# Loads, square roots and transposes of the first chunk rearranged in a fused layer-norm, S5 and SwiGLU kernel

## The chip, the cores and the metric

The kernel runs on one core of one Trainium2 chip. The metric is the device time of one execution in microseconds (us), and lower is better. Before the change it takes 180.79 us (median of 3 runs, 180.5 to 180.87).

Engine names follow the profile. PE is TensorE (the matmuls), PEld is its weight load, DVE is VectorE, ACT is ScalarE, POOL is GpSimd and SP is SyncE, which here only issues DMAs.

## The reference, cut to what matters

```python
x  = A_x                      # 1 x 2048 x 512, bf16
xn = (x - mean) / sqrt(var + 1e-5)            # layer norm over the 512 columns
# S5: a diagonal complex state-space model with 512 states
Bu = xn @ B_bar.T                             # complex
h[t] = Lam_bar * h[t-1] + Bu[t]               # scan over the 2048 rows
a  = 2 * real(h @ C.T) + xn * Dskip
# SwiGLU with 1376 hidden columns
b  = (silu(xn @ w_gate) * (xn @ w_up)) @ w_down
return x + a + b
```

All arrays are bf16. Nothing can start before some rows of x are normalised and transposed, and the first matmuls also need `w_gate`. The subject here is how this start is arranged, and what a start that comes half a microsecond sooner is worth 170 us later.

## The kernel before

The rows are cut into 4 chunks of 512, and each chunk into 4 tiles of 128 rows. Chunk 0 is special. Its tiles are normalised in halves of 256 columns, each half is transposed on PE, ACT copies it out of PSUM, and the gate matmuls of six column tiles follow tile by tile ("quarters"). Every later chunk is normalised as a whole and transposed by DMA. The weights have 512 rows, which the matmuls sum over; a K slice is 128 of these rows.

A list scheduler in the program fixes the order of ACT, DVE and POOL ahead of time. An `order=` argument forces one task behind another. PE and SP keep the order of the program. The traces show DVE and ACT keeping to their lists: in the kernel before ACT's square root of tile 1, whose data were ready at 6.09, came at 6.52, behind two evacuations.

The loads, the layer norm of chunk 0, its transposes and its gate matmuls:

```python
x_load(0)                                          # 128 KB, SP
act_q = [x_load(1, eng="act")]                     # ACT's first DMA issue
act_q.append(wg_load(0, eng="act", order=(act_q[-1],)))   # gate weights, K slices 0 and 1, 384 KB
x_load(2)
wg_load(1)                                         # K slices 2 and 3
x_load(3)
...  # [cut] parameters, w_up, the rest of w_gate, x tiles 4-7

def ln_chunk0():
    last = bn_half(0, 0)                           # statistics of 256 columns
    for a in range(4):
        last = bn_half(a, 1, order=(last,))
        last = g.add("dve", ... bn_aggr ..., order=(last,))
        hold["sd"] = g.add("act", ... Sqrt(var + eps) ...)
        if a < 3:
            last = bn_half(a + 1, 0, order=(last,))
        last = g.add("dve", ... reciprocal(sd0) -> rstd ..., order=(last,))
        for h in range(2):
            last = ln_half(a, h, order=(last,))    # xn = (x - mean) * rstd, 256 columns
    ...  # [cut]

def xt_tile_fine(a, hs=(0, 1)):
    for h in hs:
        ...  # [cut] PE: two 128 x 128 transposes of xn
        ...  # [cut] ACT: copy of 128 x 256 from PSUM to xnT ("evacuation")

def ffn_gate_quarters(pairs):
    ...  # [cut]
    pe_warm(10, 512, wbank)                        # matmuls on constants ("warm-up")
    ln_chunk0()
    xt_tile_fine(0, (0,)); pe_warm(1, 256, wbank)
    xt_tile_fine(0, (1,)); pe_warm(3, 128, wbank)
    for q in range(4):                             # tile q of the chunk
        if q < 3:
            steps = [(i, bk, 2 * kh, 2 * kh + 2) for kh in range(2) for i, bk in tiles]
        ...  # [cut]
        for n, (i, bk, k0, k1) in enumerate(steps):
            if q < 3 and n in (8, 10):             # transposes of the next tile
                xt_tile_fine(q + 1, ((n - 8) // 2,))
            ...  # [cut] params_t at q == 3, n == 4; then the matmuls of this step
```

Part of the later chunks:

```python
def loads_stage_b2():
    dma("ld_cre", CT[:, 0], A_C_re, ..., xpose=True)      # the program lets a transposing load wait for all DMAs before it,
    dma("ld_cim", CT[:, 1], A_C_im, ..., xpose=True)      # and every later load wait for it
    dma("ld_x8", x_sb[:, 8:12, :], ...)                   # x tiles 8-11, that is chunk 2
    ...  # [cut] w_down, x tiles 12-15, Dskip

def ln_apply_act(a0):                                     # chunks 2 and 3
    g.add("dve", ... nmr = -mean * rstd ...)              # rstd comes from POOL
    for a in range(a0, a0 + 4):
        g.add("act", ... xn = rstd * x + nmr ...)         # four ACT instructions of 0.7 us
```

## Time and profile before

| reading (profiled run, 180.54 us) | before |
|---|---|
| span, PE busy | 178.8 us, 174.8 us (98%) |
| x0 and x1 land | 3.34, 3.53 us |
| first gate weight piece lands (its last landing record) | 6.61 us |
| first gate matmul starts | 6.75 us |
| normalisation of tiles 0, 1, 2, 3 starts on DVE | 4.92, 7.04, 8.78, 10.52 us |
| first 512-wide matmul starts (called F below) | 13.37 us |
| last matmul of the kernel starts | 176.25 us |

Part 1 and part 4 of the page (busy time of each engine with its share of the span and its instructions; then the chain that ended last, by engine):

```profile
span 178.8 us, 2391 instructions
PE 174.8 (98%) x917; PEld 83.6 (47%) x925; DVE 161.9 (91%) x280; ACT 89.5 (50%) x116; POOL 9.9 (6%) x21
...
PE 95%; DMA 1%; DVE 1%; issue 1%; ACT 0%
```

PE is the bound, and it is nearly full. The only time to be had lies where PE is not yet at its work, in the first 13 us. The chain of waits, cut to that stretch, has the start, the duration and what was done; its last line continues to 20 us:

```profile
0.79 2.54 DMA x_sb<-in_A_x_dram
...
6.24 0.39 ACT xnT L552
6.64 0.11 issue
6.75 1.05 PE pb L760 x16
...
13.54 6.47 PE pb L715 x30
```

Read naively, it says that the first gate matmul at 6.75 waited for ACT's evacuation. The timeline of the same stretch (start, duration, engine, line, operation, output from input, and in brackets the idle time before and what ended it) is more exact:

```profile
4.72 0.16 DVE L519 RECIPROCAL rstd<-sd 128x1 f32<-128x1 f32 x1
...
5.82 0.81 ACT L552 ACTIVATE xnT<-pb 128x256 bf16<-128x256 bf16 x2 [1.13 <-PE pb L546]
...
6.52 0.29 ACT L515 ACTIVATE sd<-mv,epst 128x1 f32<-128x1 f32 x1
...
6.75 0.55 PE L760 MATMUL pb<-xnT,wg 128*128 128x128 bf16 x7 [0.22 <-ACT xnT L552]
...
7.04 0.34 DVE L505 TENSOR_SCALAR xn_sb<-x_sb,mv,rstd 128x256 bf16<-128x256 bf16 x1
```

The gate matmuls of chunk 0 end where the first 512-wide matmul starts:

```profile
13.37 5.34 PE L715 MATMUL pb<-xnT,wu 128*128 128x512 bf16 x24
```

Two things are to be seen. The two evacuations began at 5.82, and the first of them is all that the first matmuls need. It ended at 6.20, and they started at 6.75. And ACT did the square root of tile 1 (6.52) only behind both evacuations, so the normalisation of tile 1 began at 7.04, 2.12 us behind that of tile 0.

What else arrived late was the weights. The trace has 16 landing records for the first weight piece, read here as one for each of the 16 DMA engines, in us:

```
4.68 4.70 4.71 4.73 4.74 4.75 4.77 4.78 4.79 4.81 4.82 4.83 4.85 4.92   6.13   6.61
```

Fourteen of them lie at 4.92 or before, and the last two came 1.2 and 1.7 us later. PE's first gate matmul started at 6.75, behind the last of the 16 records (6.61) and not behind the fourteenth (4.92), although the evacuation that it needs had ended at 6.20.

### The profile page before, as it was taken

How to read it: one execution, taken by the hardware profiler on the slowest of the kernel's cores; microseconds unless marked ns; L12 is line 12 of the kernel's file. 1: busy time of each engine (PE TensorE's matmuls, PEld its weight loads, DVE VectorE, ACT ScalarE, POOL GpSimd, SP SyncE). 2: the span in 40 equal slices, each digit the busy share in tenths (PEclk: the TensorE clock that was granted, in tenths of full speed). 3: DMA queues.
4: the chain of work that ended last, by engine and by line, in shares of the span. 5: the costliest groups of instructions: out<-in, count | busy, mean ns of one | idle time of the engine just before them, and what ended most of it. 6: DMA issues, size and time to landing. Idle time of an engine off the chain costs nothing.

```text
span 178.8 us, 2391 instructions
## 1 busy us (share of the span) xinstructions
PE 174.8 (98%) x917; PEld 83.6 (47%) x925; DVE 161.9 (91%) x280; ACT 89.5 (50%) x116; POOL 9.9 (6%) x21
## 2 busy tenths in 40 slices
PE   8999999999999999999999999999999999999994
PEld 2694444443444444444444444444444444444743
DVE  2859884798799999999999999999999999999983
ACT  3469898989899947006655651000965620000000
POOL 3013400001300000040000000000000000000000
PEclk9999999999999999999999999999999999999999
DMA  5994669469460000002330000001100000000122
GB/s 177 350 340 110 87 134 107 90 172 354 123 117 4 0 0 0 0 4 87 78 71 0 0 0 4 0 0 59 59 0 4 0 0 0 0 0 4 59 86 90
DMA packets 22882, 12.37 MB, mean 69 GB/s; under 512 B 15096, under 2 KB 22872, under 8 KB 22872
## 3 DMA queue, kind: packets, MB, share of 16 engines
q1 hardware_dynamic: 22456, 11.70, 25.4%
q10 hardware_dynamic: 416, 0.52, 0.9%
q8 instruction: 7, 0.11, 0.3%
q14 instruction: 3, 0.02, 0.0%
HBM read 6.46 MB, written 2.10 MB: 48 GB/s over the span
## 4 chain that ended last, share of the span: by engine, by line
PE 95%; DMA 1%; DVE 1%; issue 1%; ACT 0%
PE pb L715 36%; PE pb L915 21%; PE pb L832 15%; PE pb L928 15%; PE pb L760 3%; PE pb L795 2%; DMA x_sb<-in_A_x_dram 1%; PE pb L805 1%; PE pb L546 1%; DVE st L500 0%; ACT xnT L552 0%; DVE xn_sb L505 0%; ACT sd L515 0%; DVE x_sb L933 0%; DVE mv L513 0%
## 5 line engine op out<-in xcount | busy, mean ns | idle before, releaser
L872 DVE TENSOR_TENSOR_SCAN rot<-sm,car,rot 128x512 bf16<-128x512 f32 x32 | 39.0, 1266 | 0.1
L915 PE MATMUL pb<-wd,hT 128*128 128x512 bf16 (+3 forms) x194 | 38.1, 355 | 0.2
L715 PE MATMUL pb<-xnT,wu 128*128 128x512 bf16 x160 | 37.3, 379 | 0.0
L715 PE MATMUL pb<-xnT,wg 128*128 128x512 bf16 x136 | 32.0, 379 | 0.0
L928 PE MATMUL pb<-W,hss 128*128 128x512 bf16 (+2 forms) x140 | 28.1, 355 | 0.2
L832 PE MATMUL pb<-xnT,BT 128*128 128x512 bf16 x128 | 28.1, 379 | 0.0
L915 PEld LDWEIGHTS pb<-wd,hT 128*128 128x128 bf16 (+1 forms) x198 | 18.5, 98 | 19.9
L715 PEld LDWEIGHTS pb<-xnT,wu 128*128 128x128 bf16 x160 | 15.6, 98 | 18.7 <-ACT uf L785 0.3
L727 ACT ACTIVATE sg<-pb 128x1024 bf16<-128x1024 f32 x20 | 20.2, 1023 | 7.7 <-PE pb L715 7.6
L785 ACT ACTIVATE uf<-pb 128x1024 bf16<-128x1024 f32 x20 | 20.4, 1026 | 7.0 <-PE pb L715 5.3
L715 PEld LDWEIGHTS pb<-xnT,wg 128*128 128x128 bf16 x136 | 13.2, 98 | 16.4 <-issue 0.8
L928 PEld LDWEIGHTS pb<-W,hss 128*128 128x128 bf16 x144 | 13.4, 98 | 14.3
L832 PEld LDWEIGHTS pb<-xnT,BT 128*128 128x128 bf16 x128 | 12.5, 98 | 15.1
L839 ACT ACTIVATE u_sb<-pb 128x1024 bf16<-128x1024 f32 x16 | 16.4, 1025 | 4.9 <-PE pb L832 4.5
L787 DVE TENSOR_TENSOR hT<-sg,uf 128x1024 bf16<-128x1024 bf16 x20 | 13.3, 677 | 0.4 <-ACT uf L785 0.3
L863 DVE TENSOR_TENSOR rot<-u_sb,cosT 128x2048 bf16<-128x2048 bf16 x8 | 9.7, 1216 | 2.9 <-ACT cosT L676 2.9
L933 DVE TENSOR_TENSOR x_sb<-pb,x_sb 128x512 bf16<-128x512 f32 (+2 forms) x18 | 10.8, 623 | 1.4 <-PE pb L928 1.4
L814 ACT ACTIVATE sg<-pb 96x1024 bf16<-96x1024 f32 x2 | 2.0, 1020 | 17.3 <-PE pb L795 17.3
L494 ACT ACTIVATE xn_sb<-x_sb,nmr,rstd 128x512 bf16<-128x512 bf16 x8 | 5.9, 803 | 8.9 <-DVE nmr L491 8.9
L863 DVE TENSOR_TENSOR rot<-rot,cosT 128x2048 bf16<-128x2048 bf16 x8 | 9.7, 1215 | 0.1
L863 DVE TENSOR_TENSOR rot<-rot,sin 128x2048 bf16<-128x2048 bf16 x8 | 9.7, 1216 | 0.0
L863 DVE TENSOR_TENSOR rot<-u_sb,sin 128x2048 bf16<-128x2048 bf16 x8 | 9.7, 1214 | 0.0
(76 smaller groups left out, 143.0 us busy)
## 6 DMA issues: line engine op xcount, KB each, us to landing
out_dram<-x_sb SPq DMA_DIRECT2D x15, 128.0 KB, 1.7
x_sb<-in_A_x_dram SPq DMA_DIRECT2D x3, 512.0 KB, 7.5
wd<-in_B_w_down_dram SPq DMA_DIRECT2D x1, 1280.0 KB, 7.0
wu<-in_B_w_up_dram SPq DMA_DIRECT2D x1, 768.0 KB, 5.6
wg<-in_B_w_gate_dram SPq DMA_DIRECT2D x1, 608.0 KB, 6.9
wu<-in_B_w_up_dram SPq DMA_DIRECT2D x1, 608.0 KB, 8.0
x_sb<-in_A_x_dram SPq DMA_DIRECT2D x3, 128.0 KB, 2.7
wg<-in_B_w_gate_dram ACTq DMA_DIRECT2D x1, 384.0 KB, 5.4
```

The lines of the kernel that those rows point to most:

```text
L494: g.add("act", lambda e, a=a: e.activation(out=xn_sb[:, a % NXN, :], in_=x_sb[:, a, :], func=AF.Identity, scale=rstd[:, a:a + 1], bias=nmr ...
L715: inst = e.matmul(pbank[0:fs, bk, :].rearrange("p (j t) -> p j t", j=4), lhsT=w[:, kt, i * 128:i * 128 + fs], rhs=xnT[:, c % 2, :, kt, :], ...
L727: g.add("act", lambda e: e.activation(out=sg[rows, sl, 0:n, :].rearrange("p a t -> p (a t)"), in_=pair_f32(rows, bk, 512 * n), func=AF.Sil ...
L785: g.add("act", lambda e: e.activation(out=uf[rows, ul, 0:n, :].rearrange("p a t -> p (a t)"), in_=pair_f32(rows, bk, 512 * n), func=AF.Ide ...
L787: g.add("dve", lambda e: e.tensor_tensor(out=hT[rows, hb, i0:i0 + n, :], in0=sg[rows, sl, 0:n, :], in1=uf[rows, ul, 0:n, :], op=ALU.mult), ...
L832: inst = e.matmul(pbank[:, bk, :].rearrange("p (j t) -> p j t", j=4), lhsT=BT[:, ri, kt, pt * 128:(pt + 1) * 128], rhs=xnT[:, c % 2, :, kt ...
L839: g.add("act", lambda e: e.activation(out=u_sb[:, us].rearrange("p r t -> p (r t)"), in_=pair_f32(slice(0, 128), b0), func=AF.Identity), r ...
L863: tt = lambda out, a, b, op, r, w, nm: g.add("dve", lambda e: e.tensor_tensor(out=out, in0=a, in1=b, op=op), reads=r, writes=w, name="%s_% ...
L872: g.add("dve", lambda e, A0=A0, A1=A1, k=k, ri=ri, pt=pt: e.tensor_tensor_scan(out=A1[:, k, ri, :], data0=rr[:, pt:pt + 1].to_broadcast([1 ...
L915: inst = e.matmul(pbank[:, bk, 0:nc_], lhsT=hT[0:fs, hb, i, lt * 128:(lt + 1) * 128], rhs=wd[0:fs, i, c0:c0 + nc_], start=(i == 0), stop=F ...
L928: inst = e.matmul(pbank[:, bk, 0:nc_], lhsT=hss[:, hb, pt, ri, lt * 128:(lt + 1) * 128], rhs=W12[:, ri, pt, c0:c0 + nc_], start=False, sto ...
L933: g.add("dve", lambda e, bk=bk, a=a, c0=c0, nc_=nc_: e.tensor_tensor(out=x_sb[:, a, c0:c0 + nc_], in0=pbank[:, bk, 0:nc_], in1=x_sb[:, a, ...
```

## The change

The change is meant to start the gate matmuls sooner and to keep DVE, ACT and PE from waiting for each other in chunk 0. Its parts are these.

- Loads: SP issues x0, x1 and x2, one after the other. The weights come in three K pieces of 384, 192 and 192 KB. ACT first issues a tiny load (the "touch", a few values from 16 partitions of the weights) and then the first two pieces; SP issues the third, behind x2.
- Tile 0 gets its statistics in one pass of 512 columns, not two of 256. The loop around it is only written differently.
- The square root of the next tile stands ahead of the evacuation of the second half.
- The transposes of tiles 2 and 3 come two steps earlier among the gate matmuls, and those of tile 1 are placed for the three K pieces.
- The transpose of the parameters moves into tile 3's transposes, and its copy from DVE to ACT.

```diff
-        x_load(0)
-        act_q = [x_load(1, eng="act")]
-        act_q.append(wg_load(0, eng="act", order=(act_q[-1],)))
-        x_load(2)
-        wg_load(1)
+        x_load(0)
+        x_load(1)
+        act_q = [dma("ld_touch", tch[0:16], wg_v[0:128:8, :, 0:2], [("tch",)], 16 * 16, eng="act")]
+        act_q.append(wg_load("a0", 0, 2, eng="act", order=(act_q[-1],)))
+        x_load(2)
+        act_q.append(wg_load("a1", 2, 3, eng="act", order=(act_q[-1],)))
+        wg_load("a2", 3, 4)
         x_load(3)
 ...
         def ln_chunk0():
-            last = bn_half(0, 0)
+            last = ln_stat0(0, (bn_full(0),))           # 512-wide pass, aggregate, square root
+            last = bn_half(1, 0, order=(last,))
             for a in range(4):
-                last = bn_half(a, 1, order=(last,))
-                ... bn_aggr, Sqrt, bn_half(a + 1, 0) ...
                 last = ... reciprocal ...
                 for h in range(2):
                     last = ln_half(a, h, order=(last,))
+                if a < 3:
+                    last = bn_half(a + 1, 1, order=(last,))
+                    last = ln_stat0(a + 1, (last,))     # aggregate, square root
+                if a < 2:
+                    last = bn_half(a + 2, 0, order=(last,))
 ...
                 hold["evac"] = g.add("act", evac, ...,
+                                     order=(hold["sd%d" % (a + 1)],) if h and a < 3 else ())
 ...
-            pe_warm(10, 512, wbank)
+            pe_warm(9, 512, wbank)
+            pe_warm(2, 128, wbank)
 ...
-                    if q < 3 and n in (8, 10):
-                        xt_tile_fine(q + 1, ((n - 8) // 2,))
+                    if q < 3 and n in ((12, 15) if q == 0 else (6, 8)):
+                        xt_tile_fine(q + 1, (0 if n in (6, 12) else 1,))
 ...  # [cut] the parameter transposes, and a repair of the scheduler's priorities
```

More of the change, by code (lines that the diff above doesn't have):

```diff
@@ L90, in _schedule @@
         t.lat = (_DMA_LAT + t.nbytes / _DMA_BW) if t.dma else 0.0
-    for t in reversed(tasks):
+    nin = defaultdict(int)
+    for t in tasks:
+        for d in succ[t]:
+            nin[d] += 1
+    for d in chain_next.values():
+        nin[d] += 1
+    topo = [t for t in tasks if nin[t] == 0]
+    for t in topo:
+        for d in succ[t] + ([chain_next[t]] if t in chain_next else []):
+            nin[d] -= 1
+            if nin[d] == 0:
+                topo.append(d)
+    for t in reversed(topo):
         b = 0.0
@@ L319, in bass_parallel_sum__ssm_conv_s5__swiglu_ffn__prompt_kernel @@
         epst = sb("epst", [128, 1], F32)
+        tch = sb("tch", [16, KT, 2], B16)
         praw = sb("praw", [128, 3, PT], B16)
@@ L396, in bass_parallel_sum__ssm_conv_s5__swiglu_ffn__prompt_kernel, with pload, wg_load @@
         FH0 = 6 * 128
-        def pload(name, slot, src):
-            return dma(name, prow[4 * slot:4 * slot + 4, :], src.rearrange("(a p) -> a p", p=128), [("prow", slot)], 1024)
+        def pload(name, slot, src, **kw):
+            return dma(name, prow[4 * slot:4 * slot + 4, :], src.rearrange("(a p) -> a p", p=128), [("prow", slot)], 1024, **kw)
         def x_load(a, **kw):
             return dma("ld_x%d" % a, x_sb[:, a:a + 1, :], x_v[:, a:a + 1, :], [("x", a)], TILEB, **kw)
-        def wg_load(h, **kw):
-            return dma("ld_wgA%d" % h, wg[:, 2 * h:2 * h + 2, 0:FH0], wg_v[:, 2 * h:2 * h + 2, 0:FH0], [("wg", "a%d" % h)], 256 * FH0 * 2, **kw)
+        def wg_load(nm, k0, k1, **kw):
+            return dma("ld_wg" + nm, wg[:, k0:k1, 0:FH0], wg_v[:, k0:k1, 0:FH0], [("wg", nm)], (k1 - k0) * 128 * FH0 * 2, **kw)
         x_load(0)
-        act_q = [x_load(1, eng="act")]
-        act_q.append(wg_load(0, eng="act", order=(act_q[-1],)))
+        x_load(1)
+        act_q = [dma("ld_touch", tch[0:16], wg_v[0:128:8, :, 0:2], [("tch",)], 16 * 16, eng="act")]
+        act_q.append(wg_load("a0", 0, 2, eng="act", order=(act_q[-1],)))
         x_load(2)
-        wg_load(1)
+        act_q.append(wg_load("a1", 2, 3, eng="act", order=(act_q[-1],)))
+        wg_load("a2", 3, 4)
         x_load(3)
@@ L459, in pe_warm @@
             g.add("pe", mm, writes=BK(bk), name="pe_warm", est=n * w * 0.84, ninst=n)
-        def params_t(slot):
-            g.add("pe", lambda e: e.transpose(out=ptr[:, slot, 0:12], in_=prow[:], identity=ident[0:12, 0:12]),
-                  reads=[("prow", k) for k in range(3)] + [("ident",)], writes=BK(slot), name="parT", est=60)
-        def params_ev(slot, order):
-            return g.add("dve", lambda e: e.tensor_copy(out=praw[:].rearrange("p k a -> p (k a)"), in_=ptr[:, slot, 0:12]),
-                         reads=BK(slot), writes=[("praw", k) for k in range(3)], name="parTev", est=80, order=order)
         def bn_st(a, order=()):
@@ L500, in bn_half @@
             return g.add("dve", lambda e: e.bn_stats(out=st0[:, a, h, :], in_=x_sb[:, a, h * 256:(h + 1) * 256]),
-                         reads=[("x", a)], writes=[("st0", a, h)], name="bnst%d_%d" % (a, h), est=330, order=order)
+                         reads=[("x", a)], writes=[("st0", a, h)], name="bnst%d_%d" % (a, h), est=350, order=order)
         def ln_half(a, h, order=()):
@@ L505, in ln_half @@
             return g.add("dve", lambda e: e.tensor_scalar(out=xn_sb[:, a % NXN, cs], in0=x_sb[:, a, cs], scalar1=mv[:, a, 0:1], scalar2=rstd[:, a:a + 1],
-                                                          op0=ALU.subtract, op1=ALU.mult),
-                         reads=[("x", a), ("mv", a), ("rstd", a)], writes=[("xh", a, h)] + ([("xn", a % NXN)] if h else []), name="xn%d_%d" % (a, h), est=220, order=order)
+                                                        op0=ALU.subtract, op1=ALU.mult),
@@ new lines, in ln_half, with ln_stat0 @@
+                         reads=[("x", a), ("mv", a), ("rstd", a)], writes=[("xh", a, h)], name="xn%d_%d" % (a, h), est=300, order=order)
+        def ln_stat0(a, order):
+            t = g.add("dve", lambda e: e.bn_aggr(out=mv[:, a, :], in_=st0[:, a].rearrange("p h s -> p (h s)")[:, 0:6 if a == 0 else 12]),
+                      reads=[("st0", a, 0), ("st0", a, 1)], writes=[("mv", a)], name="bnag%d" % a, est=160, order=order)
+            hold["sd%d" % a] = g.add("act", lambda e: e.activation(out=sd0[:, a:a + 1], in_=mv[:, a, 1:2], func=AF.Sqrt, bias=epst[:, 0:1]),
+                                     reads=[("mv", a), ("epst",)], writes=[("sd0", a)], name="sd%d" % a, est=280)
+            return t
@@ L509, in ln_chunk0, with bn_full @@
         def ln_chunk0():
-            last = bn_half(0, 0)
+            def bn_full(a, order=()):
+                return g.add("dve", lambda e: e.bn_stats(out=st0[:, a, 0, :], in_=x_sb[:, a, :]), reads=[("x", a)], writes=[("st0", a, 0)], name="bnst%d" % a, est=640, order=order)
+            last = ln_stat0(0, (bn_full(0),))
+            last = bn_half(1, 0, order=(last,))
             for a in range(4):
-                last = bn_half(a, 1, order=(last,))
-                last = g.add("dve", lambda e, a=a: e.bn_aggr(out=mv[:, a, :], in_=st0[:, a].rearrange("p h s -> p (h s)")),
-                             reads=[("st0", a, 0), ("st0", a, 1)], writes=[("mv", a)], name="bnag%d" % a, est=130, order=(last,))
-                hold["sd"] = g.add("act", lambda e, a=a: e.activation(out=sd0[:, a:a + 1], in_=mv[:, a, 1:2], func=AF.Sqrt, bias=epst[:, 0:1]),
-                                   reads=[("mv", a), ("epst",)], writes=[("sd0", a)], name="sd%d" % a, est=280)
-                if a < 3:
-                    last = bn_half(a + 1, 0, order=(last,))
@@ L519, in ln_chunk0 @@
                 last = g.add("dve", lambda e, a=a: e.reciprocal(out=rstd[:, a:a + 1], in_=sd0[:, a:a + 1]), reads=[("sd0", a)], writes=[("rstd", a)],
-                             name="rstd%d" % a, est=100, order=(last,))
+                             name="rstd%d" % a, est=140, order=(last,))
                 for h in range(2):
                     last = ln_half(a, h, order=(last,))
+                if a < 3:
+                    last = bn_half(a + 1, 1, order=(last,))
+                    last = ln_stat0(a + 1, (last,))
@@ L541, in xt_tile_fine, with tr2 @@
                 slot = xt_pair[0] + h
-                def tr2(e, h=h, slot=slot):
+                par = a == 3 and h == 1
+                def tr2(e, h=h, slot=slot, par=par):
+                    if par:
+                        e.transpose(out=ptr[:, slot, 512:524], in_=prow[:], identity=ident[0:12, 0:12])
                     for j in range(2):
@@ L548, in tr2 @@
                     return inst
-                g.add("pe", tr2, reads=[("xh", a, h), ("ident",)], writes=BK(slot), name="xT%d_%d" % (a, h), est=2 * 64, ninst=2)
+                g.add("pe", tr2, reads=[("xh", a, h), ("ident",)] + [("prow", k) for k in range(3) if par], writes=BK(slot), name="xT%d_%d" % (a, h), est=2 * 64 + 100 * par, ninst=2 + par)
                 def evac(e, h=h, slot=slot):
@@ L553, in evac @@
                                         in_=ptr[:, slot, 0:256].rearrange("p (k t) -> p k t", k=2), func=AF.Identity)
-                hold["evac"] = g.add("act", evac, reads=BK(slot), writes=[("xnTh", a, h)] + ([("xnT", 0, a % 4)] if h else []), name="xTev%d_%d" % (a, h), est=340)
+                if par:
+                    g.add("act", lambda e, slot=slot: e.activation(out=praw[:].rearrange("p k a -> p (k a)"), in_=ptr[:, slot, 512:524], func=AF.Identity),
+                          reads=BK(slot), writes=[("praw", k) for k in range(3)], name="parTev", est=200, order=(hold["evac"],))
+                hold["evac"] = g.add("act", evac, reads=BK(slot), writes=[("xnTh", a, h)] + ([("xnT", 0, a % 4)] if h else []), name="xTev%d_%d" % (a, h), est=340,
+                                     order=(hold["sd%d" % (a + 1)],) if h and a < 3 else ())
         def xt_chunk_dma(c):
@@ L562, in resid_chunk @@
             s0 = (4 * c) % NXN
-            xr = [("xn", s0 + j) for j in range(4)]
+            xr = [("xn", s0 + j) for j in range(4)] + ([("xh", j, h) for j in range(4) for h in range(2)] if c == 0 else [])
             xx = [("x", 4 * c + j) for j in range(4)]
@@ L700, in wres @@
             if nm == "wg" and i < 6:
-                return [("wg", "a0"), ("wg", "a1")]
+                return [("wg", "a0"), ("wg", "a1"), ("wg", "a2")]
             return [(nm, 0 if i < 6 else 1)]
@@ L749, in ffn_gate_quarters @@
             for q in range(4):
-                if q < 3:
+                if q == 0:
+                    steps = [(i, bk, 0, 2) for i, bk in tiles] + [(i, bk, k, k + 1) for k in (2, 3) for i, bk in tiles]
+                elif q < 3:
                     steps = [(i, bk, 2 * kh, 2 * kh + 2) for kh in range(2) for i, bk in tiles]
@@ L762, in mm @@
                         return inst
-                    hs = range(k0 // 2, k1 // 2)
-                    if q == 3 and n == 4:
-                        params_t(xt_pair[0])
-                        params_ev(xt_pair[0], (hold["xn3"],))
-                    g.add("pe", mm, reads=[("wg", "a%d" % h) for h in hs] + [("xnTh", q, h) for h in hs], writes=BK(bk), name="mm_gq%d_%d_%d" % (i, q, k0),
+                    hs = range(k0 // 2, (k1 + 1) // 2)
+                    g.add("pe", mm, reads=[("wg", "a%d" % max(k - 1, 0)) for k in range(k0, k1)] + [("xnTh", q, h) for h in hs], writes=BK(bk), name="mm_gq%d_%d_%d" % (i, q, k0),
                           est=(k1 - k0) * 56, ninst=k1 - k0)
```

## The prediction

> **What bounds the kernel now.** Page, part 1: PE is busy 174.8 of 178.8 us (98%). The chain of waits is 95% PE; the list of PE's waits shows none after 20 us. So only the start can be shortened. The timeline: first gate matmul at 6.75, first up matmul at 13.54 by the chain, and from there PE runs back to back to the end.
>
> **What gates the first matmul.** The chain names ACT's evacuation of xnT (6.24 + 0.39). I doubt this: the first gate matmuls need only the first half, and that evacuation began at 5.82 and took 0.384. The landing records of the first weight load (384 KB, issued on ACT at 1.22) say something else: 14 of its 16 DMA engines finish by 4.92, one at 6.13 and one at 6.61; PE's semaphore event follows at 6.64. At the end its packets trickle beside the other queue's. [...] So the gate is the weight's last two engines, at 6.6.
>
> **What the change does.**
> 1. Loads. x1 moves to SyncE, a tiny touch takes ACT's first issue (0.4 us), so weights still start near 1.2; K slices 2 and 3 are split (192 KB each), slice 2 behind slices 0 and 1 in the same queue. Fewer bytes on SyncE compete with the first piece: I expect it at 4.9 to 5.9.
> 2. Tile 0 statistics in one 512-wide pass: 0.615 (later chunks: 2.46 for four) for 0.76, and a shorter aggregate: 0.2 us sooner. From the trace's steps: normalised half 4.71, transpose 5.2, evacuation 5.61 to 5.99, first matmul about 6.1, 0.65 sooner, if the weights are there.
> 3. Square root of tile 1 ahead of the second evacuation: before it waited from 6.09 to 6.52 for ACT. Tile 1's xn starts at about 6.44, was 7.04. The second half of xnT is ready at 6.5, needed at 6.8.
> 4. Transposes two steps earlier in tiles 1 and 2: DVE needs 1.74 us per tile (7.56 to 9.30), PE 1.65, so PE now meets DVE: two stalls of about 0.1.
> 5. Parameter transpose: the same PE work (0.11); its copy moves to ACT. Parameters come about 1 us sooner; off the critical path.
>
> **What is lost.** PE steps at 6.0 to 6.3 are still 107 ns for 128 columns, at 6.75 they are 56. [...] Matmuls moved to 6.1 may run the first 0.2 to 0.5 us at half speed: minus 0.1 to 0.25.
>
> **Sum.** 0.65 (start) - 0.15 (clock) - 0.1 (meeting DVE) = 0.4 to 0.6 us. What follows has enough lead: BT's second transpose lands at 23.6 and is needed at 25.5; scan results and W are done at 73.9, needed at 75.8. So the gain should reach the end in full: 180.79 - 0.5 = 180.3 us, range 179.65 to 180.8. This is 0.3%: chance of faster by over 2% 0.01, within 2% 0.98, slower 0.01.
>
> **What would show it.** First gate matmul at 6.0 to 6.3; first weight piece before 6; second square root before the second evacuation; first 512-wide matmul at 12.8 to 13.1; the rest shifted as a block.
>
> **What would make it wrong.** The first piece keeps late engines and lands at 6.6 again (gain near 0); a later K slice is late; a new order of DVE work makes PE wait; or the late engines are an accident of that run, and ordinary runs had less to gain.

The three terms come to 0.65 - 0.15 - 0.1 = 0.4 us, the low end of the 0.4 to 0.6, and the time was predicted with 0.5. The 0.15 (clock) is the estimate from the steps of 107 and 56 ns in the trace of the kernel before.

## More of the kernel before

All runs that are compared here are at a granted TensorE clock of 0.99 or more.

One more stretch of the profile before matters later. At 47 to 50 us ACT normalises chunk 2 and then evacuates an up tile:

```profile
40.99 2.47 DVE L470 BATCH_NORM_STATS2 st<-x_sb 128x6 f32<-128x512 bf16 x4 [0.75 <-DMA x_sb<-in_A_x_dram]
...
46.77 2.93 ACT L494 ACTIVATE xn_sb<-x_sb,nmr,rstd 128x512 bf16<-128x512 bf16 x4 [0.64 <-DVE nmr L491]
...
49.61 1.00 ACT L785 ACTIVATE uf<-pb 128x1024 bf16<-128x1024 f32 x1
```

The statistics of chunk 2 start when its load lands (40.97), and ACT's four normalisations stand ahead of the evacuation at 49.61. PE did not stop for this in the kernel before.

## The result, and the profile after

The kernel after takes 180.26 us (median of 4 runs, 179.93 to 180.52), and the kernel before took 180.72 us in the same rounds (4 runs, 180.5 to 180.87). The ratio is 0.9974, with a 95% interval of 0.9954 to 0.9995. A ratio here is always the one for the fast runs of the same rounds. It is not quite the ratio of the medians that are quoted, nor that of plain means (for e11 those give 0.9989).

| reading (profiled run, 179.93 us) | before | after |
|---|---|---|
| x0 and x1 land | 3.34, 3.53 | 3.06, 3.96 |
| first gate weight piece lands | 6.61 | 4.82 |
| first gate matmul starts | 6.75 | 5.89 |
| normalisation of tiles 0, 1, 2, 3 starts | 4.92, 7.04, 8.78, 10.52 | 4.56, 6.30, 8.04, 9.78 |
| F, first 512-wide matmul | 13.37 | 12.65 |
| last matmul starts | 176.25 | 175.63 |

The page after, part 1 and part 4:

```profile
span 178.2 us, 2394 instructions
PE 174.2 (98%) x918; PEld 83.5 (47%) x926; DVE 162.0 (91%) x278; ACT 89.4 (50%) x117; POOL 9.6 (5%) x21
...
PE 95%; DMA 1%; DVE 1%; issue 1%; ACT 0%
```

The chain of waits after, over the same stretch:

```profile
0.79 2.27 DMA x_sb<-in_A_x_dram
...
5.36 0.39 ACT xnT L571
5.75 0.14 issue
5.89 1.17 PE pb L786 x18
...
7.61 0.03 issue
7.64 0.84 PE pb L786 x12
...
12.81 7.34 PE pb L738 x34
```

The timeline after:

```profile
3.99 0.43 DVE L507 BATCH_NORM_STATS2 st<-x_sb 128x6 f32<-128x256 bf16 x1
4.36 0.16 DVE L529 RECIPROCAL rstd<-sd 128x1 f32<-128x1 f32 x1
...
5.36 0.38 ACT L571 ACTIVATE xnT<-pb 128x256 bf16<-128x256 bf16 x1 [1.03 <-PE pb L565]
...
5.77 0.29 ACT L519 ACTIVATE sd<-mv,epst 128x1 f32<-128x1 f32 x1
5.89 1.17 PE L786 MATMUL pb<-xnT,wg 128*128 128x128 bf16 x18 [0.17 <-ACT xnT L571]
5.97 0.36 ACT L571 ACTIVATE xnT<-pb 128x256 bf16<-128x256 bf16 x1
...
6.30 0.60 DVE L512 TENSOR_SCALAR xn_sb<-x_sb,mv,rstd 128x256 bf16<-128x256 bf16 x2
```

Later in the same profile stand the reciprocal of tile 3, and F:

```profile
9.58 0.16 DVE L529 RECIPROCAL rstd<-sd 128x1 f32<-128x1 f32 x1 [0.36 <-ACT sd L519]
...
12.65 5.34 PE L738 MATMUL pb<-xnT,wu 128*128 128x512 bf16 x24
```

The square root (5.77) now lies between the two evacuations, and tile 1's normalisation starts at 6.30, no longer at 7.04. All 16 landing records of the first weight piece lie between 4.15 and 4.82, so now it really is the evacuation (its end at 5.74) that the first gate matmul (5.89) waits for.

Then look at 50 us:

```profile
40.45 2.47 DVE L477 BATCH_NORM_STATS2 st<-x_sb 128x6 f32<-128x512 bf16 x4 [0.94 <-DMA x_sb<-in_A_x_dram]
...
46.20 2.93 ACT L501 ACTIVATE xn_sb<-x_sb,nmr,rstd 128x512 bf16<-128x512 bf16 x4 [1.30 <-DVE nmr L498]
...
49.03 1.00 ACT L808 ACTIVATE uf<-pb 128x1024 bf16<-128x1024 f32 x1
```

PE runs 0.72 us sooner than before from F on. This evacuation comes only 0.58 us sooner (49.61 to 49.03), because it stands behind the load of chunk 2. PE now waits there: between two matmuls the start-to-start step is 0.09 us longer than the usual 0.216. Before it was not. Of the 0.72 us at F, 0.62 us are left at the last matmul, and the span is 0.6 us shorter.

So two questions are left for experiments. Which part of the change made F earlier, and what takes some of the gain back at 50 us?

### The profile page after: what moved, and what is told of

The parts are those of the page before. It is cut to its first block, busy times and chain, and to the rows that moved or that the text cites. A ratio compares the mean times of both kernels' runs of the same rounds, so it can differ in the third digit from the quotient of the medians.

```text
span 178.2 us, 2394 instructions
## 1 busy us (share of the span) xinstructions
PE 174.2 (98%) x918; PEld 83.5 (47%) x926; DVE 162.0 (91%) x278; ACT 89.4 (50%) x117; POOL 9.6 (5%) x21
## 4 chain that ended last, share of the span: by engine, by line
PE 95%; DMA 1%; DVE 1%; issue 1%; ACT 0%
PE pb L738 36%; PE pb L938 21%; PE pb L855 16%; PE pb L951 15%; PE pb L786 3%; PE pb L818 2%; DMA x_sb<-in_A_x_dram 1%; PE pb L828 1%; PE pb L565 1%; DVE st L525 0%; DVE st L507 0%; ACT xnT L571 0%; DVE xn_sb L512 0%; DVE x_sb L956 0%; DVE mv L517 0%
## 5 line engine op out<-in xcount | busy, mean ns | idle before, releaser
L738 PEld LDWEIGHTS pb<-xnT,wg 128*128 128x128 bf16 x136 | 13.1, 98 | 16.4 <-issue 0.8
```

The source lines that it names most:

```text
L738: inst = e.matmul(pbank[0:fs, bk, :].rearrange("p (j t) -> p j t", j=4), lhsT=w[:, kt, i * 128:i * 128 + fs], rhs=xnT[:, c % 2, :, kt, :], ...
```

## The experiments

Twelve kernels were run. All gave correct results. Each was timed against the kernel before on the same chip; where the text says "profile", it means the one profiled run of that kernel. By the order of instructions in the traces, the list scheduler also moved some DVE or ACT work elsewhere in the program in all but e3, e4 and e5, which is a limit of these edits.

### e1: the change with the old loads

```diff
 # against the kernel after
-        x_load(1)
-        act_q = [dma("ld_touch", ...)]
+        act_q = [x_load(1, eng="act")]
         act_q.append(wg_load("a0", 0, 2, eng="act", order=(act_q[-1],)))
         x_load(2)
-        act_q.append(wg_load("a1", 2, 3, ...))
-        wg_load("a2", 3, 4)
+        wg_load("a1", 2, 4)
```

> The kernel after with the load order of before (x1 first on ACT, weights in two pieces, no touch). If the weights gate the first matmul (my theory): the first piece has two late engines and lands at 6.4 to 6.8, the first gate matmul is at 6.5 to 6.8, the first 512-wide matmul at 13.3 to 13.5, and the time is that of before, 180.6 to 180.8 us. If the normalisation chain gates (the rival, as the chain of waits named it): first gate matmul at 6.1, first 512-wide at 12.9, time 180.3, little lost.

Measured: 180.41 us, ratio 0.9996 (0.9984 to 1.0008) to the kernel before, which had 180.45 in this group of runs. No gain. In the profile the first weight piece landed at 5.43, not at 6.61, although it is issued as in the kernel before. The second piece landed at 7.05 instead, and PE stopped for it:

```profile
7.19 0.49 PE L784 MATMUL pb<-xnT,wg 128*128 128x128 bf16 x6 [0.20 <-DMA wg<-in_B_w_gate_dram]
```

The compute part of the change gains nothing on the old loads. And which piece of the weights is late differs from run to run.

### e2: the new loads alone

```diff
 # against the kernel before
+        # the load block of the kernel after, three K pieces; matmuls wait for the pieces they read
```

> The kernel before with the new loads alone. Weights gate: x0 lands at 3.1, first piece at 4.8, first gate matmul at 6.0 (the evacuation of the first half at 5.9 is then the gate), first 512-wide matmul at 12.8 to 12.9, so nearly all of the gain: 180.2 to 180.4 us. Normalisation chain gates: only the 0.28 us by which x0 is sooner is gained, first gate matmul at 6.45.

Measured: 180.28 us, ratio 0.9989 (0.9976 to 1.0002). This is less than half the gain and not clear of zero. The profile has x0 at 3.06, as after, and the first gate matmul at 6.32, 0.43 us sooner than before. But F is 13.19, only 0.18 us sooner. The second surprise is x1, which now comes third and landed at 4.34:

```profile
4.36 0.43 DVE L503 BATCH_NORM_STATS2 st<-x_sb 128x6 f32<-128x256 bf16 x1 [0.28 <-DMA x_sb<-in_A_x_dram]
4.71 0.15 DVE L522 RECIPROCAL rstd<-sd 128x1 f32<-128x1 f32 x1
```

DVE's list has half of tile 1's statistics ahead of tile 0's reciprocal. So tile 0, whose data came 0.28 us sooner, waited for tile 1's data, and its reciprocal was at 4.71 as before (4.72).

### e3: the change without the touch

```diff
-        act_q = [dma("ld_touch", ...)]
-        act_q.append(wg_load("a0", 0, 2, eng="act", order=(act_q[-1],)))
+        act_q = [wg_load("a0", 0, 2, eng="act")]
```

> The kernel after without the touch, so the first weight piece is issued at 0.79 beside x0. Theory (x0 alone is what brings it 0.28 us sooner): x0 lands at 3.3 to 3.7, all of the normalisation chain shifts by that, first gate matmul at 6.1 to 6.5, time 180.4 to 180.8. Rival (the touch only warms the queue, order does not matter): x0 at 3.1, first gate matmul at 5.9, time 180.2.

Measured: 181.78 us, ratio 1.0073 (1.0055 to 1.0090), slower than before, and by far more than the expectation allowed for. The weights start 0.4 us sooner, and the x tiles land later: x0 at 3.44 (after: 3.06) and x1 at 4.83 (after: 3.96).

```profile
4.85 0.43 DVE L506 BATCH_NORM_STATS2 st<-x_sb 128x6 f32<-128x256 bf16 x1 [0.48 <-DMA x_sb<-in_A_x_dram]
5.20 0.14 DVE L528 RECIPROCAL rstd<-sd 128x1 f32<-128x1 f32 x1
...
5.87 0.37 PE L564 MATMUL pb<-ident,xn_sb 128*128 128x128 bf16 x2 [0.82 <-DVE xn_sb L511]
...
6.80 2.10 PE L785 MATMUL pb<-xnT,wg 128*128 128x128 bf16 x18
```

PE stood idle between its warm-up and the first transpose, and then the 18 gate matmuls took 2.10 us; in the kernel after the same 18 took 1.17 us. The steps are 107 ns until 9.34 us, and 56 ns from there. So the delay by the touch is needed, and the touch is not a waste of ACT's time.

### e4: the change without the order on the square roots

```diff
-                                     order=(hold["sd%d" % (a + 1)],) if h and a < 3 else ())
+                                     order=())
```

> The kernel after with the square root of tile 1 behind tile 0's second evacuation again. If it matters: tile 1's xn starts about 0.3 us later (6.6 in place of 6.30), the first transpose of tile 1 waits, tile 2 and 3 follow since DVE sets the pace, first 512-wide matmul at 12.9 in place of 12.65, time 0.2 to 0.3 us longer (180.5). If DVE had slack there: no change in the time.

Measured: 180.41 us, ratio 0.9999 (0.9986 to 1.0011). The gain is gone. The profile shows the old order on ACT:

```profile
5.68 0.66 ACT L571 ACTIVATE xnT<-pb 128x256 bf16<-128x256 bf16 x2 [1.36 <-PE pb L565]
...
6.22 0.30 ACT L519 ACTIVATE sd<-mv,epst 128x1 f32<-128x1 f32 x1
```

Tile 1 was normalised at 6.75 and F was 13.21. Not all of this is the missing order: in this run x1 also landed late (4.33, against 3.96), which put tile 0 at 4.88, where the kernel after had 4.56. From tile 0 to tile 1 it is 1.87 us here and 1.74 us after, so 0.13 us of the loss in this profile belongs to the order at tile 1. The edit takes the order away for the later tiles too, and the step from tile 2 to tile 3 is 1.86 us here against 1.74, with that square root behind both evacuations again: 0.12 us more.

### e5: the kernel after, once more

The edit is empty. The run shows how much the kernel after differs from itself.

> The kernel after unchanged, on the chip of this job, as the mark for the other three. Expected 0.3 to 0.5 us below before. x1 lands somewhere between 3.9 and 4.4, and tile 0's reciprocal follows it at 4.36 to 4.70, since the first half of tile 1's statistics stands ahead of it on DVE.

Measured: 180.14 us (179.87 to 180.36, 6 runs), ratio 0.9978 (0.9966 to 0.9990) to the kernel before at 180.54. The result repeats. Its profile is not that of the first run, though: F is 12.87 and not 12.65. The cause is PE's speed. Its steps for 128 columns were 107 ns in the first transposes and in the gate matmuls up to 6.37 us, where in the kernel after they were 56 ns from 4.6 us on:

```profile
5.98 1.22 PE L786 MATMUL pb<-xnT,wg 128*128 128x128 bf16 x16
...
46.57 2.93 ACT L501 ACTIVATE xn_sb<-x_sb,nmr,rstd 128x512 bf16<-128x512 bf16 x4 [1.46 <-DVE nmr L498]
```

At 50 us PE lost 0.24 us in this run. With F 0.50 us sooner than in the kernel before, the last matmul was only 0.25 us sooner.

### e6: tile 0's statistics in two halves again

```diff
-            last = ln_stat0(0, (bn_full(0),))
+            last = ln_stat0(0, (bn_half(0, 1, order=(bn_half(0, 0),)),))
```

> The kernel after with tile 0's statistics in two halves again. If step 2 of the prediction holds (0.2 us from the single pass): tile 0's reciprocal 0.15 to 0.2 us later than in the after of this job, and the time about 0.15 us longer. Rival (x1's landing hides it): where x1 lands at 4.2 or later, the reciprocal comes 0.36 after x1's landing in both kernels, and the time is the same within 0.05 us.

Measured: 180.01 us, ratio 0.9975 (0.9963 to 0.9988), the same as the kernel after. In the profile the reciprocal came at 4.43 (after: 4.36) and F at 12.72 (after: 12.65):

```profile
4.07 0.43 DVE L507 BATCH_NORM_STATS2 st<-x_sb 128x6 f32<-128x256 bf16 x1
4.43 0.16 DVE L529 RECIPROCAL rstd<-sd 128x1 f32<-128x1 f32 x1
```

x1 landed at 4.05 here, 0.09 us later than in the kernel after, and this alone would have brought the reciprocal to about 4.42. From the landing of x0 to the normalisation of tile 0 it is 1.58 us here and 1.49 us after. So the wide pass is worth less than 0.1 us, not the 0.2 us that the prediction gave it, and the timed runs do not show even that.

### e7: x1 made to land sooner

A second touch delays the weights once more, and the K slice 2 goes to SP.

```diff
         act_q = [dma("ld_touch", ...)]
+        act_q.append(dma("ld_touch2", tch2[0:16], ..., eng="act", order=(act_q[-1],)))
         act_q.append(wg_load("a0", 0, 2, eng="act", order=(act_q[-1],)))
         x_load(2)
-        act_q.append(wg_load("a1", 2, 3, eng="act", order=(act_q[-1],)))
+        wg_load("a1", 2, 3)
```

> The kernel after with a second touch in front of the first weight piece on ACT, so that piece is issued at 1.66 and x1 at 1.22 comes before it; K slice 2 goes to SyncE. If x1's late landing holds tile 0's reciprocal: x1 lands at 3.4 to 3.6, the reciprocal is at 4.35, the first piece lands at 5.0 to 5.5, first gate matmul at 5.85 to 5.95, and the time is 0.1 to 0.3 us below that of after. If x1 does not matter: the same time as after, or longer by what the weight piece is late.

Measured: 180.30 us, ratio 0.9981 (0.9966 to 0.9997), no better than the kernel after. The aim was reached, x1 landed at 3.58. But tile 0's reciprocal was again at 4.36, because then ACT's square root of tile 0 comes last. In this profile PE's steps were 107 ns until 6.6 us, F was 12.92, and the stall at 50 us was the longest, 0.42 us:

```profile
49.63 1.00 ACT L810 ACTIVATE uf<-pb 128x1024 bf16<-128x1024 f32 x1
...
50.69 1.69 PE L740 MATMUL pb<-xnT,wu 128*128 128x512 bf16 x7 [0.26 <-ACT uf L810]
```

### e8: no touch, but a longer warm-up

```diff
 # against e3
-            pe_warm(9, 512, wbank)
-            pe_warm(2, 128, wbank)
+            pe_warm(12, 512, wbank)
```

> The kernel without the touch, which took 1.3 us more, with 12 warming matmuls of 512 columns in place of 9 and two short ones, so that PE is busy until the first transposes. If most of the 1.3 us was the PE clock [...]: 128-column steps are 56 ns by the first gate matmul, the first gate matmul is at 6.5 to 6.8, the first 512-wide at 13.3 to 13.6, the time 180.6 to 180.9. If it was the late x0 and x1 alone: the time stays at 181.5 or above.

Measured: 181.33 us, the median of five fast runs (180.92 to 182.69), ratio 1.0056 (1.0029 to 1.0083). A sixth run, the profiled one (187.34 us), is not compared. Against e3's 1.0073 the longer warm-up recovers only a little. How the loss without the touch divides between late data and slow PE steps stays open, because the fast runs of e8 have no profile.

### e9: the kernel after, with x tiles 8 to 11 loaded before C

This one tests the stall at 50 us. The load of chunk 2 moves ahead of the two transposing loads of C.

```diff
         def loads_stage_b2():
+            dma("ld_x8", x_sb[:, 8:12, :], ...)
             dma("ld_cre", CT[:, 0], A_C_re, ..., xpose=True)
             dma("ld_cim", CT[:, 1], A_C_im, ..., xpose=True)
-            dma("ld_x8", x_sb[:, 8:12, :], ...)
```

> The kernel after with the load of x tiles 8 to 11 moved ahead of the two transposing loads of C in the SyncE queue. Theory (gain given back at 50 us): in after that load lands at 40.4 to 40.8, the four normalisations of chunk 2 on ACT come behind it and hold up an evacuation that PE waits for at 50 us (stalls of 0.09 and 0.24 in two profiles), so part of what the start gains is lost there. With the load at about 31 there is no PE stall between 42 and 58, the shift of the first 512-wide matmul against before (13.37) is found again at the last matmul within 0.05 us, and the time is 0.1 to 0.25 us below after, 179.9 on the mark of before at 180.5. Rival: the stall is from DVE or from the chain of transposes elsewhere, and the time stays or the wait appears at another place.

Measured: 180.07 us (179.92 to 180.16), ratio 0.9966 (0.9954 to 0.9978) to the kernel before at 180.62. In the profile:

```profile
30.46 2.48 DVE L477 BATCH_NORM_STATS2 st<-x_sb 128x6 f32<-128x512 bf16 x4 [1.21 <-DMA x_sb<-in_A_x_dram]
...
45.81 1.01 ACT L808 ACTIVATE uf<-pb 128x1024 bf16<-128x1024 f32 x1
...
48.84 1.02 ACT L808 ACTIVATE uf<-pb 128x1024 bf16<-128x1024 f32 x1
```

The load lands 10 us sooner, ACT does the four normalisations one at a time between other work, and there is no stall at 50 us. F was 12.97 (PE's steps of 107 ns again, until 6.42), 0.40 us sooner than before, and the last matmul was 0.40 us sooner as well. Nothing was given back.

### e10: the kernel before with the same move

This is the control for e9.

> The control: the kernel before with the same move. In before PE does not wait at 50 us (the evacuation ends 0.1 us ahead of its need), so the move alone should bring nothing: within 0.1 us of before. If it is faster by as much as after_x8 is than after, the move is a gain of its own and not the removal of the give-back.

Measured: 180.54 us, ratio 0.9991 (0.9978 to 1.0004) to 180.62. No clear gain: the move alone does nothing that these runs can tell from zero, as the kernel before has no stall there to take away. Its profile gave something that was not planned. The first weight piece landed at 5.26 and the first gate matmul started at 6.43, 0.32 us sooner than in the kernel before. Yet F was 13.39, where before it was 13.37. A sooner first matmul alone was worth nothing.

### e11: e9 with other places for the transposes

```diff
 # against e9
-                    if q < 3 and n in ((12, 15) if q == 0 else (6, 8)):
+                    if q < 3 and n in ((9, 13) if q == 0 else (8, 10)):
-                par = a == 3 and h == 1          # parameter transpose with tile 3
+                par = a == 2 and h == 1          # with tile 2, its copy behind the evacuation
```

> The kernel of e9 (after, with the load of x tiles 8 to 11 earlier) with PE's transposes where DVE and ACT are ready for them: tile 1 three steps earlier in tile 0's matmuls, tiles 2 and 3 two steps later, and the parameter transposes with tile 2 in place of tile 3. If the stalls of the gate stage (0.25, 0.14, 0.22 and 0.15 between two starts in e9, where 0.056 is the pace) come from the places of the transposes, the stage gets 0.2 to 0.35 us shorter, first 512-wide matmul at 12.4 to 12.75, all of it kept at the end: 179.8 on the mark of before at 180.55, ratio 0.995 to 0.996. If DVE's pace of 1.74 us per tile fixes the stage's end whatever the places, the time is that of e9, ratio 0.9966.

Measured: 180.60 us, ratio 0.9996 (0.9952 to 1.0040). The run with the profile is the fastest, 179.69 us, with F at 12.53. One more run had 179.74. The other four had 180.46 to 181.07. Why is open: only the fast one has a profile. The runs of the kernel before in this group include one of 182.68 us, which widens the intervals of e11 and e12. A version whose runs spread over 1.4 us is not a better one. What its profile does show is that F came 2.67 us behind the start of tile 3's normalisation, where it is 2.84 to 2.87 us in the runs above (e8 apart). Two edits could have done this, the places of the transposes and the move of the parameter transposes; they were not tried one by one.

### e12: e11 with half of the normalisation on POOL

```diff
 # against e11
                 last = ln_half(a, 0, order=(last,))
-                last = ln_half(a, 1, order=(last,))
+                if a in (1, 2): ln_half(a, 1, eng="pool")
+                else: last = ln_half(a, 1, order=(last,))
-  ... n in ((9, 13) if q == 0 else (8, 10))
+  ... n in ((9, 13) if q == 0 else (7, 10))
```

> The same with the second halves of tiles 1 and 2 normalised on POOL, which is idle there, so DVE's pace per tile falls from 1.74 to about 1.48 us and PE's own work of 1.65 is the bound. If DVE is the bound of the gate stage in e11: another 0.1 to 0.2 us, first 512-wide matmul at 12.2 to 12.5, ratio 0.9945 to 0.9955. If POOL needs over 1 us for a half (it has not been measured for this), its transposes stall PE and it is slower than e11.

Measured: 180.52 us, ratio 0.9991 (0.9952 to 1.0031), with F at 13.66 in the profile, later than before. The edit was to take 0.26 us per tile from DVE:

```profile
6.34 0.43 DVE L507 BATCH_NORM_STATS2 st<-x_sb 128x6 f32<-128x256 bf16 x1 [0.48 <-DMA x_sb<-in_A_x_dram]
...
7.02 2.73 POOL L512 TENSOR_SCALAR xn_sb<-x_sb,mv,rstd 128x256 bf16<-128x256 bf16 x2 [4.93 <-DVE rstd L529]
...
8.38 0.29 PE L568 MATMUL pb<-ident,xn_sb 128*128 128x128 bf16 x2 [0.59 <-POOL xn_sb L512]
```

POOL takes 1.29 us for a half that DVE does in 0.34, and PE's second transposes of tile 1 waited for it. In this run the load of x2 was late as well, and it held DVE at 6.34. The step from tile 1 to tile 2 was 1.52 us, the only one below 1.74; the next one, 2.28 us, took that back.

## Why the prediction was right or wrong

The time was right: 180.3 us was predicted and 180.26 us measured, inside the range and inside the 2% that had 0.98. The way there was right in part. Two steps of the sum failed, and they failed in opposite directions.

**What decided F.** The prediction said "So the gate is the weight's last two engines, at 6.6", counted from there, and gave 0.65 us for a first matmul that starts sooner. The weights did gate the first matmul in that run. They did not gate the stage. Put side by side when the normalisation of each tile starts on DVE, from the profiles (us):

| run | tile 0 | tile 1 | tile 2 | tile 3 | F | F minus tile 3 |
|---|---|---|---|---|---|---|
| before | 4.92 | 7.04 | 8.78 | 10.52 | 13.37 | 2.85 |
| after | 4.56 | 6.30 | 8.04 | 9.78 | 12.65 | 2.87 |
| e1 old loads | 4.90 | 6.64 | 8.63 | 10.37 | 13.23 | 2.86 |
| e2 loads alone | 4.89 | 6.87 | 8.61 | 10.35 | 13.19 | 2.84 |
| e3 no touch | 5.38 | 7.12 | 9.96 | 11.70 | 14.56 | 2.86 |
| e4 no order | 4.88 | 6.75 | 8.49 | 10.35 | 13.21 | 2.86 |
| e5 after again | 4.55 | 6.29 | 8.27 | 10.01 | 12.87 | 2.86 |
| e6 two halves | 4.63 | 6.38 | 8.12 | 9.86 | 12.72 | 2.86 |
| e7 x1 sooner | 4.56 | 6.30 | 8.31 | 10.06 | 12.92 | 2.86 |
| e9 after, x8 | 4.71 | 6.45 | 8.37 | 10.11 | 12.97 | 2.86 |
| e10 before, x8 | 5.20 | 7.07 | 8.81 | 10.55 | 13.39 | 2.84 |
| e11 | 4.64 | 6.38 | 8.12 | 9.86 | 12.53 | 2.67 |
| e12 half on POOL | 4.67 | 6.87 | 8.39 | 10.67 | 13.66 | 2.99 |

(e8 is not in it, since its profile is slow.) F follows tile 3's normalisation by 2.84 to 2.87 us in the first eleven rows, and no step between tiles is shorter there than 1.74 us. These 1.74 us are not DVE's work alone. They are one round through two engines: DVE normalises, takes the second half of the next tile's statistics and aggregates them, ACT takes the square root, DVE the reciprocal. In the last round DVE has no further statistics to fill the wait with and is idle for 0.36 us until the square root is there (the line at 9.58 above), and the step is 1.74 us all the same. e12 takes 0.26 us of work out of the round, and its one undisturbed step is 1.52 us. So the start of the kernel is a chain of such rounds through DVE and ACT, and what shortens it is a sooner tile 0 or a shorter step; what follows tile 3 is PE's work, which e11 shortened. The first gate matmul fits in or does not; e10 shows it with 0.32 us sooner and F unmoved. A late weight piece can still cost time by another way: in e1 PE waited for the second piece, tile 1's transposes came later, and the step from tile 1 to tile 2 was 1.99 us. In the kernel before, the PE chain from the late weights ended within about 0.1 us of the chain through DVE (transposes of tile 3 at 10.95, their data ready at 10.87), which is why the false bound gave a usable number.

Read along the rows, the 0.72 us at F come from two places: 0.36 us at tile 0, and 0.38 us between tiles 0 and 1 (2.12 to 1.74).

**Tile 0 (predicted 0.2 sooner by the wide pass).** The 0.36 us came from elsewhere. x0 landed 0.28 us sooner, 3.06 instead of 3.34, with x1 no longer issued beside it (x0 landed at 3.05 to 3.18 in all runs with a touch, and at 3.34 to 3.61 with x1 issued beside it: before, e1, e10); the prediction had not counted that. The wide pass gives 0.09: from x0's landing to tile 0's normalisation it is 1.49 to 1.50 us with it (after, e1, e7) and 1.58 without (before, e6, e10). Against this, x1 lands later than before, at 3.58 to 4.34 in the runs with a touch, and above about 4.0 it delays tile 0's reciprocal through DVE's order: 4.36 with x1 at 3.96, 4.70 with x1 at 4.33 (e4) or 4.34 (e2). That is a dependence that the prediction did not see, and it differs between runs of one kernel.

**The square root (predicted: tile 1 at 6.44).** Right, it was 6.30. With the order, the step from tile 0 to tile 1 is 1.74 us whether PE's steps are 107 or 56 ns (after, e5, e6, e7, e9). Without it, it is 1.87 us where PE's steps are 56 ns by then (e4, e10), 1.98 us in e2, where they became 56 ns at about 5.7 us, and 2.12 us where they are still 107 ns (before). So the order is worth 0.13 to 0.38 us at tile 1. Timed, e4 lost all the gain, but part of that may be its late x1, so its 0.9999 is not the price of the order alone.

**Transposes earlier, "two stalls of about 0.1".** In kind right. Between the starts of PE's matmuls after the change there is a step of 0.25 us ahead of tile 1's first gate matmul (the 7.61 and 7.64 of the chain), and 0.18 and 0.22 us before the transposes of tiles 2 and 3, where the usual step is 0.056. But these are not a price of 0.1 to take off: they are PE waiting at the pace of the chain, which sets F anyway. The stage from first gate matmul to F became longer, 6.76 instead of 6.62 us.

**The clock (predicted 0.1 to 0.25 lost).** Right in some runs. The prediction calls clock what the traces show as steps of 107 ns and, from some point on, of 56 ns for matmuls of 128 columns. In the profile of the kernel after the steps were already 56 ns at 4.6 us, and nothing was lost. In e5, the same kernel, they were 56 ns only from 6.37, and F was 0.22 us later. The table shows the way: tile 0 and tile 1 are where they were, and the step from tile 1 to tile 2 is 1.98 instead of 1.74. PE's slow matmuls bring tile 1's transposes later (7.16 instead of 6.89), ACT's evacuation with them, and the square root of tile 2 stands behind that evacuation. e7 and e9 show the same step at 2.01 and 1.92, also with PE at 107 ns (until 6.6 and 6.42). e3 is the extreme: 2.84 us. Of its F, 1.19 us later than before, 0.08 us is there at tile 1, and 1.10 us is that step.

**"So the gain should reach the end in full."** This step was wrong. The prediction checked the leads of BT, the scan and W (a load and two results of the S5 part), and missed chunk 2. From F to the last matmul is 162.88 us where PE never stalls, and longer where it does. The stall at 50 us follows from when the load of x tiles 8 to 11 lands, compared with F:

| run | x8 lands | minus F | stall at 50 us | F to last matmul |
|---|---|---|---|---|
| before | 40.97 | 27.60 | 0 | 162.88 |
| after | 40.43 | 27.78 | 0.09 | 162.99 |
| e1 | 40.65 | 27.42 | 0 | 162.88 |
| e5 | 40.81 | 27.94 | 0.24 | 163.13 |
| e6 | 40.03 | 27.31 | 0 | 162.88 |
| e7 | 41.02 | 28.10 | 0.42 | 163.31 |
| e9 | 30.44 | 17.47 | 0 | 162.88 |

Above 27.69 us every tenth is a tenth of stall; e2, at 27.68, has none. The kernel before had 0.09 us of slack there. The load lands at the end of a chain of transposing loads that the program makes serial, and when PE starts sooner, that load does not follow it: against before, it came 0.54 us sooner in the kernel after, where F was 0.72 sooner, 0.16 in e5 (F 0.50), and 0.94 in e6 (F 0.65), which has no stall. Then DVE's statistics, POOL's power, `nmr`, four ACT normalisations and the evacuation follow in order, and PE waits for the evacuation. e9 takes the cause away and the stall is gone, with F to last matmul back at 162.88; e10 shows that the same move alone gains nothing clear. So this cause is shown, and not only argued.

**The sum.** In profiled runs the gain at F was 0.72 (after), 0.50 (e5) and 0.45 us (e7, a variant), and at the last matmul 0.62, 0.25 and 0.02. The timed medians differ by 0.46 us in the first group and by 0.40 us with e5. The predicted 0.5 us is near because a larger gain at the start (0.72 with PE at 56 ns from 4.6 us) and an unforeseen loss at 50 us went against each other, and because the false bound lay within a tenth of the true one. That the sum came out so close is luck. F itself, predicted at 12.8 to 13.1, was at 12.65 (after) and 12.87 (e5). The prediction's last fear, that the late engines were an accident of that run, was justified: with the old load order the first piece landed at 6.61, 5.43 and 5.26 (before, e1, e10). It did not matter, since that piece was not the bound.

**The best version.** e9 is clearly better than the kernel before (0.9966). Against the kernel after, its interval overlaps those of both measurements (0.9974 and 0.9978), so it is not shown to be better, though the mechanism that it removes is.

## What to carry to other kernels

The last event before the first matmul is not the bound of a stage: line up the starts of the same step for tile after tile, on every engine, and look for the step whose interval never gets shorter and from whose last tile the end keeps a constant distance. Then see through which engines one round of it passes; here one of them is idle for part of it. When a start is moved by half a microsecond, ask which later transfers do not move with it, and compute the slack of each; a slack of 0.09 us looks like no wait at all in the profile before. Where an engine works through its list in order, as DVE and ACT do here, an instruction that needs a later tile's data should not stand ahead of one that needs only the earlier tile's (in e2 x0 landed 0.28 us sooner and the reciprocal of tile 0 did not move, 4.71 against 4.72; no run here tried the other order).

## What these runs show of the hardware

- PE's speed at the start: the first matmul starts at 0.83 us, and with the same warm-up (apart from the last few matmuls) PE's steps went from long (107 ns for 128 columns, 427 for 512) to short (56 and 216 ns) at about 3.5 us in one run (e4), at 4.2 in another (e6), between 6.3 and 6.7 in others (before, e5, e7, e9), and only at 9.34 in e3. That is 2.7 to 5.9 us after the first matmul without e3. In the late ones PE was idle for 0.1 to 0.4 us ahead of its first transposes. In e3 PE was idle there for 1.0 us, and the steps after it were 107 ns, until 9.34. In e4 it was idle for 1.2 us with the steps already at 56 ns, and they stayed there. What sets the moment is not shown. The granted clock of the profile does not tell the two apart: it reads 1.00 from 0 to 6 us in the kernel before, where the steps are long.
- The order of issue: a small load's landing went with that order and with what ran beside it. x1 landed at 3.53 to 3.80 from ACT ahead of the weights (before, e1, e10), at 3.89 to 4.34 from SP beside the weights (after, e2, e4, e5, e6, e9, e11, e12), and at 4.83 without the touch (e3), where x0 also came 0.38 us later than after (3.44, not 3.06).
- Landing records of one load: of the first weight piece, issued from ACT, 2 of the 16 records came 1.2 and 1.7 us behind the rest (before), and not in every run of the same order of loads.
- POOL against DVE: for a half of this normalisation (128 x 256, bf16) POOL took 1.29 us and DVE 0.34 us (e12), a factor of 3.8.
